# Attention and MLP on one core: the scores of the 64 left-over keys of two pairs in quarters of the TensorE array in full float32, with one sigmoid; copies of x by two engines, stores one step later

## The chip, the cores and the metric

The kernel runs on 1 core of one Trainium2 chip. The metric is the device time of one execution, in microseconds (us). TensorE (PE) does matmuls, with its weight loads shown apart as PEld; VectorE is DVE, ScalarE is ACT, GpSimd is POOL, and SyncE (SP) issues every DMA of this kernel, in one queue.

## The reference, cut to what matters

```python
def _attn_ref(q, k, v):                     # q, k, v: (8, 12, 448, 64) float32
    S = q.shape[2]
    scale = 1.0 / np.sqrt(q.shape[-1])
    scores = scale * np.matmul(q, k.transpose(0, 1, 3, 2)) - np.log(S)
    attn = 1.0 / (1.0 + np.exp(-scores))    # sigmoid, no row sum
    return np.matmul(attn, v).astype(np.float32)

def _moe_ref(x, w_in, w_out):               # x: (3584, 768), from the heads side by side
    h = x @ w_in                            # (768, 2048)
    r = np.maximum(h, 0.0)
    g = r * r
    return (g @ w_out).astype(np.float32)   # (2048, 768)
```

## The kernel before

The work has two stages. The first is the attention of 8 x 12 heads, taken two heads at a time: 48 pairs (b, p), numbered n = 0 to 47. The second is the two matrix products of the MLP, in four groups of two batches (`gemm1`, `gemm2`, lines 398 and on); each group splits its operands into blocks and multiplies seven combinations of them in place of eight. The order of all instructions is the order of the code: nothing is rescheduled, and every engine takes its instructions in that order.

**One pair.** `load_pair` brings q and k of both heads, transposed, into one tile x of 128 partitions: 64 rows of head 0 and 64 rows of head 1, then a half with the 448 queries and a half with the 448 keys. `split_pair` (lines 200 and 201) makes from it on DVE a rounded copy qh and the remainder ql. `scores` takes the 448 keys in blocks of 128, so three blocks (t = 0 to 2) and one of 64 left-over keys (t = 3; KR = 64). For each block line 215 issues three products (qh with qh, ql with qh, qh with ql) for each of the two heads. Head j uses the array's rows j x 64 to j x 64 + 63, so that the products of the two heads can run beside each other. Then one ACT instruction (line 223) turns the block of both heads into sigmoids. For t = 3 only 64 partitions are used, and the sigmoids go into one half of a tile `rest` that two neighbouring pairs share. The score tiles rotate through three PSUM buffers (`bufs=3`), so the fourth block of a pair needs the buffer of its first.

`attn_v` (line 231) multiplies the sigmoids of the three full blocks with v in full float32, head j into the output columns j x 64 and on. `attn_v_rest` (line 240) adds the left-over keys of two pairs at once: four products of 64 rows by 64 columns, one in each quarter of the array, again in full float32. Its result stands in a PSUM tile `pav`, of which there are two, one for the even and one for the odd pair. `put_x` copies pav to SBUF (line 249 on DVE, line 247 on ACT, which before the change only the very last pair uses) and returns the store to DRAM (line 253). For the first two batches (KEPT = 2) there is no store, the copy is kept.

**One step n.** `step(ps, n)` issues, in this order: the load of pair n + 4 (and of v for two pairs when n is even); when n is even, the copies of pairs n - 2 and n - 1 and their stores; the split of pair n + 2; the scores of pair n + 1; attn_v of pair n; when n is odd, attn_v_rest of pairs n - 1 and n; then a piece of the weights' work. So each even step on PE begins with the scores of an odd pair, straight after an attn_v_rest, and each odd step with the scores of an even pair.

**The weights' work** runs beside the attention. `weights(k)` is called for k = 0 to 48, spread over steps 0 to 44, twice in steps 0, 11, 22 and 33. A third of the calls hold `sums` (lines 155 to 158 on DVE, then two stores, lines 160 and 161), two thirds `convert_join` (lines 139, 140 and 143 on DVE, line 146 on POOL) and two thirds `convert_words` (lines 134 and 135 on ACT). From step 28 on, `PIECES` adds operands of the first MLP group (lines 259, 260 and 285).

Of the kernel before, what the change touches and what calls it, by code (L numbers as in the profile page):

```python
# [8 lines left out]
F32 = mybir.dt.float32  # L9
# [4 lines left out]
AF = mybir.ActivationFunctionType  # L14
# [3 lines left out]
B, H, S, D = 8, 12, 448, 64  # L18
DM, DFF = H * D, 2048
P = 128  # L20
NP = H // 2

NT, KR = S // P, S % P
# [5 lines left out]
SCALE = 1.0 / math.sqrt(D)  # L29
NEG_LOG_S = -math.log(S)  # L30
# [28 lines left out]
def sigmoid_attention_relu2_mlp(  # L59
# [42 lines left out]

    nc = tc.nc

    sb = ctx.enter_context(tc.tile_pool(name="sb", bufs=2))

    def op2(name, dtype=F32):
        return sb.tile([P, 2, S], dtype, tag="op2", bufs=N2, name=name)  # L110

    def op1(name, dtype=F32):
        return sb.tile([P, S], dtype, tag="op1", bufs=N1, name=name)

    def wide(name, dtype=F32):
        return sb.tile([P, PH, HALF], dtype, tag="w", bufs=NW, name=name)
# [20 lines left out]
    def convert_join(t, w):  # L137
        wb = w.bitcast(I32)
        nc.vector.tensor_scalar(out=w, in0=w, scalar1=WORD_MIN, scalar2=WORD_MAX, op0=ALU.max, op1=ALU.min)
        nc.vector.tensor_scalar(  # L140
            out=wb, in0=wb, scalar1=3, scalar2=0x3FFFFFFF, op0=ALU.logical_shift_left, op1=ALU.bitwise_and
        )
        nc.vector.scalar_tensor_tensor(  # L143
            out=wb, in0=t.bitcast(I32)[:, :, 1], scalar=-(1 << 30), in1=wb, op0=ALU.bitwise_and, op1=ALU.bitwise_or
        )
        nc.gpsimd.tensor_tensor(out=wb, in0=wb, in1=t.bitcast(I32)[:, :, 0], op=ALU.add)  # L146

    def sums(m, i, a, s):

        if m == 0:  # L150
            a21, a22, a11, a12 = (a[:, n] for n in range(4))
        else:
            a22, a12, a11, a21 = (a[:, n] for n in range(4))
        s2, s3, s4, s1 = (s[:, n] for n in range(4))
        nc.vector.tensor_add(out=s1, in0=a21, in1=a22)
        nc.vector.tensor_sub(out=s2, in0=s1, in1=a11)
        nc.vector.tensor_sub(out=s3, in0=a11, in1=a21)
        nc.vector.tensor_sub(out=s4, in0=a12, in1=s2)
        to = (w1, w2)[m][i]
        nc.sync.dma_start(out=to[:, 0:3], in_=a[:, 1:4] if m == 0 else a[:, 0:3])  # L160
        nc.sync.dma_start(out=to[:, 3:7], in_=s)

    def load_weights(sources, name):

# [28 lines left out]
    def load_v(b, d):  # L193
        vt = op2(f"v_{b}_{d}").rearrange("p a s -> p (a s)").rearrange("p (t d) -> p t d", d=P)
        nc.sync.dma_start(out=vt, in_=v[b, d])
        return vt
# [4 lines left out]
        nc.vector.tensor_sub(out=lo, in0=x, in1=hi.bitcast(F32))  # L201
        return hi, lo

    def scores(ps, b, p, x, rest):


        out = []
        for t in range(NT + 1):
            sc = ps.tile([P, 2, 512], F32, tag="sc", bufs=3, name=f"sc_{b}_{p}_{t}")[:, :, :S]
            keys = P if t < NT else KR  # L210
            ks = slice(t * P, t * P + keys)
            for n, (kp, qp) in enumerate(((0, 0), (1, 0), (0, 1))):
                for j in range(2):
                    rows = slice(j * D, (j + 1) * D)
                    nc.tensor.matmul(  # L215
                        sc[:keys, j], x[kp][rows, 1, ks], x[qp][rows, 0], start=(n == 0), stop=(n == 2)
                    )
            if t < NT:
                at = op2(f"at_{b}_{p}_{t}")
                out.append(at)  # L220
            else:
                at = rest[p % 2 * KR : (p % 2 + 1) * KR]
            nc.scalar.activation(at, sc[:keys], AF.Sigmoid, bias=NEG_LOG_S, scale=SCALE)  # L223
        return out

    def attn_v(ps, b, p, at, vt):
        pav = ps.tile([P, 512], F32, tag="pav", bufs=2, name=f"pav_{b}_{p}")[:, :S]
        for t in range(NT):
            for j in range(2):
                columns = slice(j * D, (j + 1) * D)  # L230
                nc.tensor.matmul(  # L231
                    pav[columns], vt[:, p % 2 * NT + t, columns], at[t][:, j], start=(t == 0), stop=False
                )
        return pav
# [9 lines left out]
    def put_x(b, p, pav, scalar=False):  # L244
        x = op1(f"xo_{b}_{p}")
        if scalar:
            nc.scalar.copy(out=x, in_=pav)
        else:
            nc.vector.tensor_copy(out=x, in_=pav)  # L249
        if b < KEPT:  # L250
            kept[b, p] = x
            return lambda: None
        return lambda: nc.sync.dma_start(out=xd[b, p], in_=x)
# [69 lines left out]
    pairs = [(b, p) for b in range(B) for p in range(NP)]  # L323
    last = len(pairs) - 1
    todo = [(m, i) for m in range(2) for i in range(NI)]
    x, vt, xs, at, pav, f64, w, rest = {}, {}, {}, {}, {}, {}, {}, {}
    stores = []
    pieces = {}
    ops = {}

    def weights(k):

        j, h = divmod(k, 3)
        if h == 0 and j > 0:
            sums(*todo[j - 1], *w[j - 1])
        if j == len(todo):
            return
        if h == 0:  # L340
            w[j] = wide(f"a_{j}"), wide(f"s_{j}")
        halves = w[j][0].rearrange("p a n -> p (a n)")
        halves = halves[:, DM:], halves[:, :DM]
        if h > 0:
            convert_join(f64[j, h - 1], halves[h - 1])
            if j + 1 < len(todo):
                f64[j + 1, h - 1] = load_chunk(*todo[j + 1], h - 1)
        if h < 2:
            convert_words(f64[j, h], halves[h])
# [3 lines left out]
    def step(ps, n):  # L353

        if n + XA <= last:
            x[n + XA] = load_pair(*pairs[n + XA])
            if n % 2 == 0:
                b, p = pairs[n + XA]
                vt[n // 2 + XA // 2] = load_v(b, p // 2)
        if n % 2 == 0 and n > 0:  # L360
            for m in (n - 2, n - 1):
                store = put_x(*pairs[m], pav.pop(m))
                if n <= last - 3:
                    store()
                else:
                    stores.append(store)
        if n + SA <= last:
            xs[n + SA] = split_pair(*pairs[n + SA], x[n + SA])
        if n < last:
            next_scores(ps, n + 1)  # L370
        pav[n] = attn_v(ps, *pairs[n], at[n], vt[n // 2])
        if n % 2:
            attn_v_rest((pav[n - 1], pav[n]), rest[n // 2], vt[n // 2])
        for k in range(NK):
            if k * NWP // NK == n:
                weights(k)
        pieces_of(*PIECES.get(n, ()))

    def next_scores(ps, n):
        if n % 2 == 0:  # L380
            rest[n // 2] = op2(f"rest_{n // 2}")
        at[n] = scores(ps, *pairs[n], xs[n], rest[n // 2])

    def pieces_of(*names):
        for name in names:
            pieces[name]()
# [261 lines left out]
```

## Time and profile before

| | |
|---|---|
| runs of the kernel before, median | 1108.82 us (1104.78, 1108.82, 1116.4) |
| the profiled execution, own time | 1108.67 us |
| its span, first to last instruction | 1106.9 us |
| attention, first score product to first MLP product | 5.99 to 280.84 us |
| granted TensorE clock | 1.00 throughout |

The span leaves 1.8 us of the execution's own time outside. "Busy" of PE is modelled from the starts of the matmuls, so a busy PE is not one at its peak. In a timeline row the first number is the start in us from the beginning of the span, the second how long the row took, x the number of instructions merged, and brackets tell of idle time before it and what ended it. A matmul in full float32 shows as two records, so the four products of line 240 are x8.

### The profile page before, as it was taken

Reading aid. Unit: us, or ns where it says so; the run is one execution under the profiler, and the core shown is the slowest. Engines: PE = TensorE matmul, PEld = TensorE weight load, DVE = VectorE, ACT = ScalarE, POOL = GpSimd, SP = SyncE. Lnnn points to the kernel's source line nnn. Section 1 sums busy time; section 2 is a strip of 40 time slices with the busy share of each in tenths; the row PEclk is TensorE's granted clock in tenths of the full one; section 3 lists DMA queues with packets and bytes.
Section 4 is the critical chain, followed back from the end, with each engine's and each line's share of the span. In section 5 each row is a group of like instructions: output and inputs, shape, how many; then the busy total and the mean of one; then the engine's idle time right before and its main releaser. Section 6 shows DMA issues by size and latency. Waiting matters only on the chain.

```text
span 1106.9 us, 15055 instructions
## 1 busy us (share of the span) xinstructions
PE 1094.7 (99%) x5965; PEld 893.6 (81%) x5965; DVE 798.2 (72%) x879; ACT 617.0 (56%) x745; POOL 63.4 (6%) x36
## 2 busy tenths in 40 slices
PE   9999999999999999999999999999999999999998
PEld 4455544445799999999999999999999999999997
DVE  6888898999655699744558977355798945459951
ACT  6788788887534546533435655333556633346630
POOL 1222222221000000000000000000000000000000
PEclk9999999999999999999999999999999999999999
DMA  8879998897232433653233355423443642233441
GB/s 318 331 283 361 355 360 322 315 367 286 67 122 101 122 107 108 235 175 104 100 100 121 123 173 198 136 100 100 136 124 125 215 150 100 100 115 128 139 136 53
DMA packets 80134, 196.81 MB, mean 178 GB/s; under 512 B 6336, under 2 KB 54464, under 8 KB 80064
## 3 DMA queue, kind: packets, MB, share of 16 engines
q1 hardware_dynamic: 80064, 195.85, 50.5%
q8 instruction: 47, 0.77, 0.3%
q14 instruction: 23, 0.19, 0.1%
HBM read 154.53 MB, written 41.29 MB: 177 GB/s over the span
## 4 chain that ended last, share of the span: by engine, by line
PE 91%; ACT 4%; DVE 3%; issue 1%; DMA 0%; ACTq 0%; DVEq 0%
PE oa L395 21%; PE ha L395 21%; PE ob L395 11%; PE hb L395 10%; PE sc L215 8%; PE pav L231 8%; PE hc L395 5%; PE oc L395 5%; PE pav L240 2%; ACT at L223 1%; DVE ql L201 1%; ACT rest L223 1%; ACT f L135 1%; DVE qh L200 0%; PE warm_ps L562 0%
## 5 line engine op out<-in xcount | busy, mean ns | idle before, releaser
L181 DVE TENSOR_TENSOR w_1l<-w_1l,w_1h 128x1536 fp32r<-128x1536 f32 x58 | 101.8, 1755 | 87.5 <-ACT w_1h L180 85.3
L223 ACT ACTIVATE at<-sc 128x896 f32<-128x896 f32 x144 | 121.6, 921 | 51.6 <-PE sc L215 51.4
L422 ACT COPY s<-ha 128x448 f32<-128x448 f32 x96 | 50.9, 532 | 163.7 <-PE ha L395 155.2
L231 PE MATMUL pav<-at,v 128*64 128x448 f32 x576 | 118.6, 547 | 1.1 <-DVE xo L249 1.1
L180 ACT CAST w_1h<-w_1l 128x1536 fp32r<-128x1536 f32 x58 | 85.9, 1480 | 23.8 <-DMA w_1l<-w 23.7
L231 PEld LDWEIGHTS pav<-at,v 128*64 128x64 f32 x576 | 37.2, 136 | 63.2 <-issue 58.7
L215 PE MATMUL sc<-qh 64*128 64x448 f32 (+1 forms) x384 | 77.2, 399 | 4.7 <-ACT at L223 4.7
L146 POOL TENSOR_TENSOR a<-a,f 128x768 int32<-128x768 int32 x32 | 63.2, 1976 | 198.6 <-DVE a L143 135.8
L215 PEld LDWEIGHTS sc<-qh 64*128 64x128 f32 (+1 forms) x384 | 33.3, 170 | 50.9 <-ACT at L223 16.3
L180 ACT CAST w_0h<-w_0l 128x1536 fp32r<-128x1536 f32 x28 | 41.5, 1481 | 55.3 <-DMA w_0l<-w 55.3
L201 DVE TENSOR_TENSOR ql<-x,qh 128x896 fp32r<-128x896 f32 x48 | 71.1, 1480 | 1.6
L455 DVE TENSOR_TENSOR g<-hb,s 128x448 f32<-128x448 f32 x32 | 19.9, 623 | 71.1 <-PE hb L395 71.1
L215 PE MATMUL sc<-qh,ql 64*128 64x448 f32 (+1 forms) x384 | 70.2, 362 | 0.3 <-DVE ql L201 0.3
L215 PE MATMUL sc<-ql,qh 64*128 64x448 f32 (+1 forms) x384 | 70.3, 362 | 0.0
L181 DVE TENSOR_TENSOR w_0l<-w_0l,w_0h 128x1536 fp32r<-128x1536 f32 x28 | 49.2, 1757 | 24.4 <-ACT w_0h L180 24.1
L180 ACT CAST w_5h<-w_5l 128x1152 fp32r<-128x1152 f32 x31 | 35.9, 1160 | 47.3 <-DMA w_5l<-w 47.2
L181 DVE TENSOR_TENSOR w_5l<-w_5l,w_5h 128x1152 fp32r<-128x1152 f32 x31 | 42.0, 1353 | 21.9 <-ACT w_5h L180 21.9
L418 DVE SCALAR_TENSOR_TENSOR g<-g 128x896 f32<-128x896 f32 x48 | 52.2, 1088 | 1.0
L223 ACT ACTIVATE rest<-sc 64x896 f32<-64x896 f32 x48 | 43.7, 909 | 0.6
L249 DVE COPY xo<-pav 128x448 f32<-128x448 f32 x47 | 27.1, 618 | 19.5 <-PE pav L240 19.5
L200 DVE CAST qh<-x 128x896 fp32r<-128x896 f32 x48 | 36.4, 759 | 5.6 <-DMA x<-qk 5.6
L511 DVE TENSOR_TENSOR o<-ob,t 128x448 f32<-128x448 f32 x24 | 14.9, 619 | 35.2 <-PE ob L395 29.0
(628 smaller groups left out, 3025.7 us busy)
## 6 DMA issues: line engine op xcount, KB each, us to landing
w_1l<-w SPq DMA_DIRECT2D x58, 768.0 KB, 4.3
x<-qk SPq DMA_DIRECT2D x48, 448.0 KB, 7.1
w_0l<-w SPq DMA_DIRECT2D x28, 768.0 KB, 4.7
f<-w_in SPq DMA_DIRECT2D x16, 768.0 KB, 7.5
w<-s SPq DMA_DIRECT2D x16, 768.0 KB, 4.2
f<-w_out SPq DMA_DIRECT2D x16, 768.0 KB, 6.9
w_5l<-w SPq DMA_DIRECT2D x31, 384.0 KB, 3.9
v<-v SPq DMA_DIRECT2D x24, 448.0 KB, 7.2
```

The source lines that it names most:

```text
L146: nc.gpsimd.tensor_tensor(out=wb, in0=wb, in1=t.bitcast(I32)[:, :, 0], op=ALU.add)
L180: nc.scalar.copy(out=hi, in_=raw)
L181: nc.vector.tensor_sub(out=lo, in0=raw, in1=hi.bitcast(F32))
L200: nc.vector.tensor_copy(out=hi, in_=x)
L201: nc.vector.tensor_sub(out=lo, in0=x, in1=hi.bitcast(F32))
L215: nc.tensor.matmul(sc[:keys, j], x[kp][rows, 1, ks], x[qp][rows, 0], start=(n == 0), stop=(n == 2))
L223: nc.scalar.activation(at, sc[:keys], AF.Sigmoid, bias=NEG_LOG_S, scale=SCALE)
L231: nc.tensor.matmul(pav[columns], vt[:, p % 2 * NT + t, columns], at[t][:, j], start=(t == 0), stop=False)
L249: nc.vector.tensor_copy(out=x, in_=pav)
L395: nc.tensor.matmul(out, a[:, c], b, start=first and n == 0, stop=last and n == 2, skip_group_check=True)
L418: nc.vector.scalar_tensor_tensor(out=t, in0=t, scalar=0.0, in1=t, op0=ALU.max, op1=ALU.mult)
L422: nc.scalar.copy(out=s, in_=banks["a", i])
```

## The change

The scores of the 64 left-over keys leave `scores`. They are computed once for two pairs, behind the scores of the odd pair, by `scores_rest`: four products, pair r into output partitions r x 64 and on, head j from rows j x 64 and on, from the unsplit x in full float32, one product each in place of three. One sigmoid over 128 partitions takes the place of two over 64. In `step` the copy of pair n - 2 goes to ACT and stays at the front, the copy of pair n - 1 stays on DVE and moves behind the weights' work. The weights' stores are issued in the step after their sums; the stores of x are issued in the odd step after their copies, and those of pairs 42 to 47 wait for a place in the first MLP group.

```diff
-        to = (w1, w2)[m][i]
-        nc.sync.dma_start(out=to[:, 0:3], in_=a[:, 1:4] if m == 0 else a[:, 0:3])
-        nc.sync.dma_start(out=to[:, 3:7], in_=s)
+
+        def store():
+            to = (w1, w2)[m][i]
+            nc.sync.dma_start(out=to[:, 0:3], in_=a[:, 1:4] if m == 0 else a[:, 0:3])
+            nc.sync.dma_start(out=to[:, 3:7], in_=s)
+
+        return store
...
-    def scores(ps, b, p, x, rest):
-
+    def sigmoid(name, sc):
+        at = op2(name)
+        nc.scalar.activation(at, sc, AF.Sigmoid, bias=NEG_LOG_S, scale=SCALE)
+        return at
+
+    def scores(ps, b, p, x):
 
         out = []
-        for t in range(NT + 1):
+        for t in range(NT):
...
+    def scores_rest(ps, d, xs):
+
+        sc = ps.tile([P, 2, 512], F32, tag="sc", bufs=3, name=f"sr_{d}")[:, :, :S]
+        for r, x in enumerate(xs):
+            for j in range(2):
+                rows = slice(j * D, (j + 1) * D)
+                nc.tensor.matmul(
+                    sc[r * KR : (r + 1) * KR, j], x[rows, 1, NT * P :], x[rows, 0], start=True, stop=True
+                )
+        return sigmoid(f"rest_{d}", sc)
...
-            sums(*todo[j - 1], *w[j - 1])
+            ready.append(sums(*todo[j - 1], *w[j - 1]))
...
+        for waiting in (ready, stores) if n % 2 and n < last - 2 else (ready,):
+            for store in waiting:
+                store()
+            waiting.clear()
         if n % 2 == 0 and n > 0:
-            for m in (n - 2, n - 1):
-                store = put_x(*pairs[m], pav.pop(m))
-                if n <= last - 3:
-                    store()
-                else:
-                    stores.append(store)
+            stores.append(put_x(*pairs[n - 2], pav.pop(n - 2), True))
...
+        if n % 2 == 0 and n > 0:
+            stores.append(put_x(*pairs[n - 1], pav.pop(n - 1)))
         pieces_of(*PIECES.get(n, ()))
 
     def next_scores(ps, n):
-        if n % 2 == 0:
-            rest[n // 2] = op2(f"rest_{n // 2}")
-        at[n] = scores(ps, *pairs[n], xs[n], rest[n // 2])
+        at[n] = scores(ps, *pairs[n], xs[n])
+        if n % 2:
+            rest[n // 2] = scores_rest(ps, n // 2, (x[n - 1], x[n]))
```

On PE, at step 18: the scores of the odd pair (b 3, p 1), the name's first numbers being b, p and the block of keys, and what follows. Before:

```order
L215 MATMUL sc_3_1_2_1290<-qh_3_1_1199 128x448 x2
L215 MATMUL sc_3_1_2_1290<-qh_3_1_1199,ql_3_1_1200 128x448 x2
L215 MATMUL sc_3_1_2_1290<-ql_3_1_1200,qh_3_1_1199 128x448 x2
L215 MATMUL sc_3_1_3_1299<-qh_3_1_1199 64x448 x2
L215 MATMUL sc_3_1_3_1299<-qh_3_1_1199,ql_3_1_1200 64x448 x2
L215 MATMUL sc_3_1_3_1299<-ql_3_1_1200,qh_3_1_1199 64x448 x2
L231 MATMUL pav_3_0_1307<-at_3_0_0_1211,v_3_0_1010 64x448 x2
```

And now, where sr_9 is the score tile of the left-over keys of pairs 18 and 19:

```order
L223 MATMUL sc_3_1_2_1187<-qh_3_1_1109 128x448 x2
L223 MATMUL sc_3_1_2_1187<-qh_3_1_1109,ql_3_1_1110 128x448 x2
L223 MATMUL sc_3_1_2_1187<-ql_3_1_1110,qh_3_1_1109 128x448 x2
L235 MATMUL sr_9_1196<-x_3_0_927 64x448 x2
L235 MATMUL sr_9_1196<-x_3_1_990 64x448 x2
L245 MATMUL pav_3_0_1203<-at_3_0_0_1120,v_3_0_929 64x448 x2
```

The six products of 64 keys behind the third block have become four, which read x itself; behind the scores of an even pair, where six stood too, nothing stands now.

On DVE, at step 20: xo are the copies of pairs 18 and 19, qh and ql the split of the pair two ahead, a_7 the weights' join. Before:

```order
L249 COPY xo_3_0_1387<-pav_3_0_1307 128x448
L249 COPY xo_3_1_1390<-pav_3_1_1362 128x448
L200 CAST qh_3_4_1393<-x_3_4_1258 128x896
L201 TENSOR_TENSOR ql_3_4_1394<-x_3_4_1258,qh_3_4_1393 128x896
L139 TENSOR_SCALAR a_7_1379<-a_7_1379 128x768
L140 TENSOR_SCALAR a_7_1379<-a_7_1379 128x768
L143 SCALAR_TENSOR_TENSOR a_7_1379<-f64_0_7_0_1254,a_7_1379 128x768
```

And now:

```order
L205 CAST qh_3_4_1280<-x_3_4_1159 128x896
L206 TENSOR_TENSOR ql_3_4_1281<-x_3_4_1159,qh_3_4_1280 128x896
L140 TENSOR_SCALAR a_7_1268<-a_7_1268 128x768
L141 TENSOR_SCALAR a_7_1268<-a_7_1268 128x768
L144 SCALAR_TENSOR_TENSOR a_7_1268<-f64_0_7_0_1155,a_7_1268 128x768
L263 COPY xo_3_1_1333<-pav_3_1_1253 128x448
```

The copy of pair 18 has left DVE, and that of pair 19 stands behind the split and the join.

On SP, at the same steps, the queue of transfers. Before:

```order
L190 DMA x_3_5_1320<-qk 128x896
L160 DMA w1<-a_6_1193 128x1152
L161 DMA w1<-s_6_1194 128x1536
L190 DMA x_4_0_1383<-qk 128x896
L195 DMA v_4_0_1385<-v 128x896
L253 DMA xd<-xo_3_0_1387 128x448
L253 DMA xd<-xo_3_1_1390 128x448
L122 DMA f64_1_0_0_1443<-w_out 128x1536
L190 DMA x_4_1_1447<-qk 128x896
```

And now:

```order
L195 DMA x_4_0_1272<-qk 128x896
L200 DMA v_4_0_1274<-v 128x896
L163 DMA w1<-a_6_1097 128x1152
L164 DMA w1<-s_6_1098 128x1536
L123 DMA f64_1_0_0_1329<-w_out 128x1536
L195 DMA x_4_1_1335<-qk 128x896
L267 DMA xd<-xo_3_0_1278 128x448
L267 DMA xd<-xo_3_1_1333 128x448
```

Loads of x and v that stood behind a store now stand ahead of it.

## Rows read from the trace of the kernel before

**Rows 1.** The page's head: busy us, share of the span, instructions

```profile
PE 1094.7 (99%) x5965; PEld 893.6 (81%) x5965; DVE 798.2 (72%) x879; ACT 617.0 (56%) x745; POOL 63.4 (6%) x36
```

**Rows 2.** Stretches: their length, each engine's busy us, PEclk, DMA share, GB/s

```profile
80.00:240.00 160.00, 156.24 (x1122) 78.77 (x1120) 145.46 (x194) 129.75 (x159) 39.99 (x21) 1.00 0.92 347
240.00:281.00 41.00, 39.57 (x279) 18.95 (x276) 35.47 (x49) 30.76 (x40) 6.04 (x3) 1.00 0.74 273
281.00:1107.00 826.00, 821.80 (x4032) 756.53 (x4031) 553.87 (x553) 394.00 (x474) 0.00 (x0) 1.00 0.39 128
```

**Rows 3.** Timeline of PE: both ends of the attention

```profile
5.99 0.47 PE L215 MATMUL sc<-qh 64*128 64x448 f32 x2
...
274.39 4.73 PE L231 MATMUL pav<-at,v 128*64 128x448 f32 x24 [0.63 <-DVE xo L249]
279.05 0.98 PE L240 MATMUL pav<-rest,v 64*64 64x448 f32 x8
280.84 0.44 PE L395 MATMUL ha<-x_0h,w_firsth 128*128 128x448 f32 x1 [0.80 <-DVE xo L249]
```

**Rows 4.** Timeline of PE: the end of step 17, steps 18 and 19

```profile
110.01 0.98 PE L240 MATMUL pav<-rest,v 64*64 64x448 f32 x8
110.92 0.47 PE L215 MATMUL sc<-qh 64*128 64x448 f32 x2
...
112.64 0.37 PE L215 MATMUL sc<-ql,qh 64*128 64x448 f32 x2
112.85 0.37 PE L215 MATMUL sc<-qh 64*64 64x448 f32 x2
...
113.26 0.36 PE L215 MATMUL sc<-ql,qh 64*64 64x448 f32 x2
113.55 2.48 PE L231 MATMUL pav<-at,v 128*64 128x448 f32 x12
115.95 0.47 PE L215 MATMUL sc<-qh 64*128 64x448 f32 x2
...
121.07 0.98 PE L240 MATMUL pav<-rest,v 64*64 64x448 f32 x8
121.98 0.47 PE L215 MATMUL sc<-qh 64*128 64x448 f32 x2
```

**Rows 5.** Waits up to 470 us: who waited for whom, us in total, times, longest

```profile
PE sc L215 <- ACT at L223: 4.7, 5, 1.5
```

**Rows 6.** Timeline of PE, DVE and ACT at the start of step 23

```profile
138.10 0.47 PE L215 MATMUL sc<-qh 64*128 64x448 f32 x2
138.43 0.56 DVE L139 TENSOR_SCALAR a<-a 128x768 f32<-128x768 f32 x1 [0.45 <-ACT a L134]
139.62 0.96 DVE L143 SCALAR_TENSOR_TENSOR a<-f,a 128x768 int32<-128x768 int32 x1
140.70 2.52 ACT L223 ACTIVATE at<-sc 128x896 f32<-128x896 f32 x3
141.15 2.63 DVE L201 TENSOR_TENSOR ql<-x,qh 128x896 fp32r<-128x896 f32 x1
141.65 0.41 PE L215 MATMUL sc<-qh 64*64 64x448 f32 x2 [1.46 <-ACT at L223]
```

**Rows 7.** The page's groups of DVE: busy, mean ns of one, idle before

```profile
L201 DVE TENSOR_TENSOR ql<-x,qh 128x896 fp32r<-128x896 f32 x48 | 71.1, 1480 | 1.6
...
L249 DVE COPY xo<-pav 128x448 f32<-128x448 f32 x47 | 27.1, 618 | 19.5 <-PE pav L240 19.5
L200 DVE CAST qh<-x 128x896 fp32r<-128x896 f32 x48 | 36.4, 759 | 5.6 <-DMA x<-qk 5.6
```

**Rows 8.** Timeline of PE, DVE, ACT: step 34's late copies, the last copy

```profile
202.49 0.47 PE L215 MATMUL sc<-qh 64*128 64x448 f32 x2
...
205.44 1.15 DVE L249 COPY xo<-pav 128x448 f32<-128x448 f32 x2
...
280.13 0.53 ACT L247 COPY xo<-pav 128x448 f32<-128x448 f32 x1 [4.70 <-PE pav L240]
```

More of the change, by code (lines that the diff above doesn't have):

```diff
@@ L202, in split_pair @@
         return hi, lo
-    def scores(ps, b, p, x, rest):
+    def sigmoid(name, sc):
[3 more added lines that the diff above has]
+    def scores(ps, b, p, x):
         out = []
-        for t in range(NT + 1):
+        for t in range(NT):
             sc = ps.tile([P, 2, 512], F32, tag="sc", bufs=3, name=f"sc_{b}_{p}_{t}")[:, :, :S]
-            keys = P if t < NT else KR
-            ks = slice(t * P, t * P + keys)
+            ks = slice(t * P, (t + 1) * P)
             for n, (kp, qp) in enumerate(((0, 0), (1, 0), (0, 1))):
@@ L215, in scores @@
                     nc.tensor.matmul(
-                        sc[:keys, j], x[kp][rows, 1, ks], x[qp][rows, 0], start=(n == 0), stop=(n == 2)
+                        sc[:, j], x[kp][rows, 1, ks], x[qp][rows, 0], start=(n == 0), stop=(n == 2)
                     )
-            if t < NT:
-                at = op2(f"at_{b}_{p}_{t}")
-                out.append(at)
-            else:
-                at = rest[p % 2 * KR : (p % 2 + 1) * KR]
-            nc.scalar.activation(at, sc[:keys], AF.Sigmoid, bias=NEG_LOG_S, scale=SCALE)
-        return out
+            out.append(sigmoid(f"at_{b}_{p}_{t}", sc))
+        return out
+    def scores_rest(ps, d, xs):
[7 more added lines that the diff above has]
+        return sigmoid(f"rest_{d}", sc)
     def attn_v(ps, b, p, at, vt):
@@ L326, in sigmoid_attention_relu2_mlp @@
     x, vt, xs, at, pav, f64, w, rest = {}, {}, {}, {}, {}, {}, {}, {}
-    stores = []
+    ready, stores = [], []
     pieces = {}
@@ L359, in step @@
                 vt[n // 2 + XA // 2] = load_v(b, p // 2)
+        for waiting in (ready, stores) if n % 2 and n < last - 2 else (ready,):
+            for store in waiting:
+                store()
+            waiting.clear()
         if n % 2 == 0 and n > 0:
-            for m in (n - 2, n - 1):
-                store = put_x(*pairs[m], pav.pop(m))
-                if n <= last - 3:
-                    store()
-                else:
-                    stores.append(store)
+            stores.append(put_x(*pairs[n - 2], pav.pop(n - 2), True))
         if n + SA <= last:
```

## The prediction

> **What bounds the kernel now.** I read the page's head first: PE is busy 99% of the span [rows 1]. Busy ends of matmuls are modelled, so I read the distances between starts instead. The table by stretches comes next [rows 2]: the granted clock is 1.00, the 2.4 GHz level, in all of them; behind 281 us nothing that the change touches is left but six stores, and PE is busy 821.8 of 826 us. So the change is worth what it does to the attention, 5.99 to 280.84 us, 274.85 us long [rows 3].
>
> Inside it I read PE's timeline for two steps [rows 4]. Step 18 starts at 110.92, step 20 at 121.98: 11.06 us for two pairs. The reader is to see start after start with hardly a hole: nine pairs of products of full blocks in 1.93 us, then the left-over keys, where two slots take 113.26 - 112.85 = 0.41, so 0.205 each; then 0.09 more than a slot until attn_v starts at 113.55; 2.40 us of attn_v; at the end of two steps 0.91 us of attn_v_rest (110.01 to 110.92). PE's own instructions are the period, and the other engines matter where they make it wait.
>
> How much is that? The stage is 274.85. From it come 46 attn_v of 2.40 and the last two, 4.66 (274.39 to 279.05); 23 attn_v_rest of 0.91 and the last with its change to the MLP, 1.79 (279.05 to 280.84). That leaves 137.1 us for the scores of 48 pairs. At 2.63 each (110.92 to 113.55) they would take 126.2. So about 10.9 us are waits, spread unevenly. The table of waits gives their main kind: PE stood five times for a sigmoid, 4.7 us together [rows 5]. One such place shows how [rows 6]: step 22 has two calls of weights, so ACT comes to the sigmoids of the next pair only at 140.70 (2.52 for three, 0.84 each), and the fourth score block, which needs the buffer of the first, starts at 141.65 after 1.46 us of idling. The block began at 138.10; undisturbed it would have got there 1.93 later.
>
> **The change part by part.** *Products of the left-over keys.* Three slots go from every pair: 3 x 0.205 = 0.61 us. Behind an odd pair four full products come. The trace has their twin: line 240 also does four products of 64 by 64 with 448 columns in float32, one in each quarter, in 0.91 us with the change to the next form [rows 4]. Even pairs: 24 x -0.61 = -14.6. Odd pairs: 24 x (0.91 - 0.61) = +7.2. Sum -7.4. Bounds: the cheapest row is that of the rounded products, two slots for four products, 0.41, which would give 12 us more; the dearest is attn_v's, six products in 2.40, 0.40 each, four in 1.60, which costs 24 x 0.69 = 16.6 more. I take 0.91, same shape and same quarters.
>
> The changeover of the array has a rule against it. From 64 by 128 to 64 by 64 the start moves 0.21 (112.64 to 112.85), a slot like any other; into attn_v it costs 0.09 [rows 4]. The Trainium skill, TensorEngine Tiling (Array Packing), section Key Properties, says that a change of tiling mode drains the engine. There is one change less in two steps now. By the rule each would cost the 0.09 of attn_v's, and the sum would be 2.2 us lower; by the row nothing.
>
> *Sigmoids and copies.* ACT loses one sigmoid of about 0.84 per two steps and gains one copy of 0.53 [rows 8]: -0.31, while the period shrinks by 0.31 as well. ACT is busy 129.75 of 160 us [rows 2], so its load stays about 81%. What matters is which waits end. An even pair has three score blocks for three buffers now, so a late sigmoid no longer stops it in its own block. The wait of rows 6, and those like it after steps 0 and 28, go. An odd pair still needs a fourth buffer, 2.02 after its start (1.93 and 0.09), and has the 0.53 copy ahead of its first sigmoid. Where ACT is late there, after the double calls of steps 11 and 33, I leave 0.7 each.
>
> DVE loses 0.62 per two steps [rows 7]. More, it loses a wait: it stood 19.5 us for attn_v_rest before those copies. Its second copy is due later: attn_v of step n + 1 needs it, at 2.93 + 2.40 + 2.02 = 7.35 us after the start T of an even step (2.93 is 2.02 with 0.91). On DVE it stands behind a split (759 + 1480 ns [rows 7]), a join (138.43 to 140.58, 2.15 [rows 6]) and takes 0.62: 5.0 if DVE is on time. Queued behind the waiting copy are the next split and the scores that read it, so DVE's order keeps PE's two-step slack. In step 22 the join waits for words of its own step: it ended at 140.58, 7.5 after that step's start at 133.07 (138.10 less 2.63 and 2.40), then 0.62: 0.8 late, charged once.
>
> *Of the 10.9 us of waits I leave 4.3*: 1.4 after the double calls, 0.8 for step 22, 0.4 in the last odd pair (0.63 before for DVE [rows 3], now for ACT), 0.4 at the start, and about 1.3 in small ones. Gain 6.6. Bounds: none goes (0), or all (10.9).
>
> *Stores and queue.* SP issues the weights' stores one step later, those of x in odd steps, six of them in the MLP. Loads that stood behind a store go ahead. I cost this at nothing: after the start DVE waits for loads of x no more (5.6 us in all [rows 7]), so an earlier load hides behind the split's place in DVE's order. What it costs if the queue fills up is a rival below. The scores also read x itself, so its buffer comes free later; the loads are two steps ahead, which covers it.
>
> Sum: -7.4 - 6.6 = -14.0. Against the profiled execution's own time, 1108.67, it gives 1094.7. The span's 1.8 us outside stay. The median of the runs, 1108.82, is the same time, so I forecast 1094.7 for that too. About 1% is what a measurement of this kernel can tell from no change; 1% is 11 us, so the line is 1097.7.
>
> **The rivals.** *The waits move instead of going.* PE gets its -7.4, and ACT, as loaded as before, stops the odd block instead. For it: the odd block keeps four tiles on three buffers and gets a copy first. Against: the buffer comes free about when wanted even in the undisturbed steps of rows 4. Time 1108.67 - 7.4 = 1101.3.
>
> *Transfers bound the middle.* From 80 to 240 us the DMA share is 0.92 [rows 2], 147 us of transfers. That stretch would get 14.0 x 160 / 274.85 = 8.1 us of the gain, and the share would be 147 / 152 = 0.97. If it can't rise above 0.92, that gain is lost: 1102.8. Against: loads leave the queue earlier.
>
> *The quarters don't run beside each other.* Two at a time is attn_v's rate: 1094.7 + 16.6 = 1111.3, no change. One at a time takes twice 1.60, that is 2.29 more than 0.91 each time: 1149.7. The row against both is line 240 with its 0.91. The Trainium skill, FP8 and Floating Point Precision, section TensorE Precision Notes, says that true float32 takes four passes through the array. By it four products, one after the other, would be sixteen slots, 3.28 us, and the change a loss of about 43 us; the 0.91 for four disagrees unless all quarters work at once.
>
> *Slower: the second copy comes too late in every even step.* Place: attn_v of the odd pair, which needs its PSUM tile. In step 34 DVE stood 2.95 late (205.44 against 202.49 [rows 8]). If it stood so always, the copy would end at 2.95 + 5.0 = 7.95, 0.6 late; with a split slowed to 2.63 in place of 1.48 [rows 6] 1.75 late. Price: 23 x 1.75 = 40, so 1135. It decides from 0.6 us per two steps, 23 x 0.6 = 14. Against: the 19.5 us that DVE stood idle at just this place.
>
> **How the numbers follow.** The forecast's chance is 0.66, with 1090 to 1099 as its own range; 0.56 of it lies below 1097.7. Waits that move 0.12, transfers 0.10, quarters 0.06, late copy 0.06. Some 0.04 of the first two would still come out below 1097.7. Faster by over 1%: 0.60; within 1%: 0.34, with the two-at-a-time case in it; slower: 0.06. The range takes in the first two rivals and ends at 1105; below it reaches to 1090, where nearly all waits go or each change of tiling costs 0.09.
>
> **What would show it.** Right: PE's starts in two steps 10.7 apart; sr tiles written by eight records within 0.98; an even pair's scores 2.02 from start to attn_v; no idling before an even pair's last block; ACT's copy directly behind attn_v_rest. Wrong: sr records in pairs 0.4 apart; attn_v waiting for line 263; DVE waiting for x; a DMA share at 1.0 through the middle with PE idle. The forecast falls if the attention ends later than about 270 us.

## The result, and the profile after

The changed kernel takes 1092.25 us (median of 6 runs) against 1108.05 (6 runs of the kernel before): the ratio is 0.985, 95% interval [0.981, 0.989], so it is faster by about 1.5%. In a second comparison it was 1092.7 (4 runs) against 1105.45 (23 runs), 0.988 [0.985, 0.991], 12.75 us. The first profiled execution of the changed kernel was a slow one, 1108.05 us with an attention of 262.19, so the rows below are from the profile taken with the second comparison; its own time is 1095.86 us, its span 1094.1.

The page's head of the changed kernel, to be read beside [rows 1]:

```profile
PE 1084.1 (99%) x5869; PEld 882.8 (81%) x5869; DVE 800.0 (73%) x856; ACT 608.5 (56%) x744; POOL 63.6 (6%) x36
```

Its table of stretches, beside [rows 2]; the attention now ends at 268 us:

```profile
80.00:240.00 160.00, 157.17 (x1120) 75.89 (x1118) 152.94 (x189) 132.59 (x170) 40.70 (x21) 1.00 0.93 350
240.00:268.00 28.00, 27.27 (x188) 12.20 (x184) 23.63 (x31) 19.11 (x26) 3.98 (x2) 1.00 0.68 250
268.00:1094.00 826.00, 821.69 (x4032) 756.70 (x4032) 553.67 (x554) 395.20 (x474) 0.00 (x0) 1.00 0.39 128
```

The MLP is as long as before, 826 us. All that was gained lies ahead of it. DVE is busier in the middle than before (152.94 against 145.46 us), and the transfers, at 0.92 before, run at 0.93.

PE's timeline of the changed kernel: the start, two steps, the end of the attention, beside [rows 3, 4].

```profile
6.12 0.54 PE L223 MATMUL sc<-qh 64*128 64x448 f32 x2
...
94.92 0.47 PE L223 MATMUL sc<-qh 64*128 64x448 f32 x2
...
96.65 0.37 PE L223 MATMUL sc<-ql,qh 64*128 64x448 f32 x2
96.94 0.98 PE L235 MATMUL sr<-x 64*64 64x448 f32 x8
97.86 2.48 PE L245 MATMUL pav<-at,v 128*64 128x448 f32 x12
100.26 0.47 PE L223 MATMUL sc<-qh 64*128 64x448 f32 x2
...
101.99 0.37 PE L223 MATMUL sc<-ql,qh 64*128 64x448 f32 x2
102.28 2.48 PE L245 MATMUL pav<-at,v 128*64 128x448 f32 x12
104.69 0.98 PE L254 MATMUL pav<-rest,v 64*64 64x448 f32 x8
105.60 0.47 PE L223 MATMUL sc<-qh 64*128 64x448 f32 x2
...
261.71 4.73 PE L245 MATMUL pav<-at,v 128*64 128x448 f32 x24
266.37 0.98 PE L254 MATMUL pav<-rest,v 64*64 64x448 f32 x8
268.16 0.44 PE L410 MATMUL ha<-x_0h,w_firsth 128*128 128x448 f32 x1 [0.80 <-DVE xo L263]
```

Two steps take 105.60 - 94.92 = 10.68 us, 11.06 before. The four products of the left-over keys (L235) stand once in them, 96.94 to 97.86, 0.92 long; an even pair's scores take 102.28 - 100.26 = 2.02. The attention lasts 268.16 - 6.12 = 262.04 us in place of 274.85: 12.81 less, and the two profiled executions differ by just that, 1108.67 - 1095.86.

I took this apart by the starts of all 48 blocks of scores, each counted up to the start of the attn_v behind it, so that a wait of that attn_v is in it too. Nothing else changed: attn_v is 110.67 us for 46 pairs in both traces. Before, the score blocks took 136.75: 48 undisturbed ones at 2.63 make 126.24, and 10.51 are waits. After, they take 123.94: 48 at 2.021 and 24 times 0.912 make 118.90, and 5.04 are waits. So the products gave 7.3 and the waits 5.5.

| waits, us | before | after |
|---|---|---|
| first two pairs | 0.58 | 0.35 |
| step 1 / 3 | 1.70 / - | - / 0.37 |
| step 12 | 0.54 | 0.63 |
| steps 23 / 25 | 1.67 / - | 0.47 / 0.25 |
| step 29 | 1.46 | - |
| steps 34 / 35 | 0.99 / 0.60 | 0.63 / 1.63 |
| step 39 | 0.44 | 0.50 |
| step 46 | 0.78 | 0.16 |
| all others, 0.13 and less each | 1.75 | 0.05 |

What DVE and PE wait for now, from the table of waits up to 470 us, beside [rows 5] (us in total, times, longest):

```profile
DVE xo L263 <- PE pav L254: 4.0, 1, 4.0
...
PE pav L245 <- DVE xo L263: 2.0, 5, 0.7
...
PE sr L235 <- ACT at L211: 1.1, 2, 0.6
```

An even pair's block stops for no sigmoid any more. In its place attn_v waits five times for the second copy. Two such places, steps 23 and 35, in the timeline of DVE, POOL and PE, the first beside [rows 6]:

```profile
132.05 0.56 DVE L140 TENSOR_SCALAR a<-a 128x768 f32<-128x768 f32 x1 [2.69 <-ACT a L135]
...
134.12 0.62 DVE L263 COPY xo<-pav 128x448 f32<-128x448 f32 x1
...
134.79 1.72 PE L245 MATMUL pav<-at,v 128*64 128x448 f32 x8 [0.40 <-DVE xo L263]
...
195.76 2.02 POOL L147 TENSOR_TENSOR a<-a,f 128x768 int32<-128x768 int32 x1 [7.50 <-DVE a L144]
196.11 2.62 DVE L206 TENSOR_TENSOR ql<-x,qh 128x896 fp32r<-128x896 f32 x1
...
198.78 0.47 PE L223 MATMUL sc<-qh,ql 64*128 64x448 f32 x2 [0.58 <-DVE ql L206]
...
200.70 0.62 DVE L263 COPY xo<-pav 128x448 f32<-128x448 f32 x1
...
201.38 2.10 PE L245 MATMUL pav<-at,v 128*64 128x448 f32 x10 [0.68 <-DVE xo L263]
```

In step 23 the copy stands behind a join that waited 2.69 us for ACT's words. In step 35 DVE is late altogether: the split's subtraction, 2.62 us long beside POOL's part of a join, stops the scores, and then the copy behind the next join stops attn_v.

The groups of DVE and ACT up to 269 us, beside [rows 7, 8]:

```profile
L206 DVE TENSOR_TENSOR ql<-x,qh 128x896 fp32r<-128x896 f32 x48 | 78.5, 1636 | 1.8
L205 DVE CAST qh<-x 128x896 fp32r<-128x896 f32 x48 | 45.7, 952 | 6.6 <-DMA x<-qk 6.6
L263 DVE COPY xo<-pav 128x448 f32<-128x448 f32 x24 | 14.8, 618 | 4.0 <-PE pav L254 4.0
L261 ACT COPY xo<-pav 128x448 f32<-128x448 f32 x24 | 12.9, 537 | 23.4 <-PE pav L254 23.4
```

The wait for attn_v_rest has moved from DVE (19.5 us) to ACT (23.4), which has the time. The split takes 1636 + 952 ns on average, 0.35 us more than before; the last section shows from what.

### The profile page after: what moved, and what is told of

It is laid out like the page before. It is cut to its first block, busy times and chain, and to the rows that moved or that the text cites. A ratio compares the mean times of both kernels' runs of the same rounds, so it can differ in the third digit from the quotient of the medians.

```text
span 1106.3 us, 14825 instructions
## 1 busy us (share of the span) xinstructions
PE 1096.6 (99%) x5869; PEld 882.7 (80%) x5869; DVE 800.9 (72%) x856; ACT 608.6 (55%) x744; POOL 63.5 (6%) x36
## 4 chain that ended last, share of the span: by engine, by line
PE 90%; DVE 5%; ACT 3%; DMA 1%; issue 0%; SPq 0%; ACTq 0%
PE oa L410 22%; PE ha L410 21%; PE ob L410 11%; PE hb L410 11%; PE pav L245 7%; PE oc L410 5%; PE hc L410 5%; PE sc L223 5%; DVE ql L206 2%; PE pav L254 1%; PE sr L235 1%; ACT at L211 1%; DMA x<-qk 1%; DVE a L144 1%; DVE qh L205 1%; DMA f<-w_out 1%
## 5 line engine op out<-in xcount | busy, mean ns | idle before, releaser
L185 ACT CAST w_1h<-w_1l 128x1536 fp32r<-128x1536 f32 x58 | 85.9, 1480 | 22.3 <-DMA w_1l<-w 22.0
L206 DVE TENSOR_TENSOR ql<-x,qh 128x896 fp32r<-128x896 f32 x48 | 78.5, 1635 | 1.8
L223 PE MATMUL sc<-qh 64*128 64x448 f32 x288 | 58.2, 401 | 0.0
L223 PEld LDWEIGHTS sc<-qh 64*128 64x128 f32 x288 | 27.0, 184 | 35.3 <-issue 12.0
L223 PE MATMUL sc<-qh,ql 64*128 64x448 f32 x288 | 52.6, 362 | 0.6 <-DVE ql L206 0.6
L433 DVE SCALAR_TENSOR_TENSOR g<-g 128x896 f32<-128x896 f32 x48 | 52.3, 1090 | 1.0
L223 PE MATMUL sc<-ql,qh 64*128 64x448 f32 x288 | 52.6, 362 | 0.0
L205 DVE CAST qh<-x 128x896 fp32r<-128x896 f32 x48 | 45.7, 952 | 5.4 <-DMA x<-qk 5.4
L464 ACT ACTIVATE g<-ha 128x448 f32<-128x448 f32 x32 | 17.4, 545 | 37.9 <-PE ha L410 37.9
L410 PE MATMUL oa<-o_0h,w_0l 128*128 128x448 f32 x96 | 35.3, 368 | 0.0
```

The source lines that it names most:

```text
L185: nc.scalar.copy(out=hi, in_=raw)
L205: nc.vector.tensor_copy(out=hi, in_=x)
L223: nc.tensor.matmul(sc[:, j], x[kp][rows, 1, ks], x[qp][rows, 0], start=(n == 0), stop=(n == 2))
L410: nc.tensor.matmul(out, a[:, c], b, start=first and n == 0, stop=last and n == 2, skip_group_check=True)
L433: nc.vector.scalar_tensor_tensor(out=t, in0=t, scalar=0.0, in1=t, op0=ALU.max, op1=ALU.mult)
```

## The experiments

The first question was which part of the change does it. Theory: the left-over scores alone. The rivals: the copies, or the stores with the order of the queue.

**e1_after**: the changed kernel as it is.

> The changed kernel as it is, for a second profile. Theory A (products of the left-over keys give 7.4 us, the ended waits for sigmoids another 6 to 9): 1092 us; attention ends near 265 to 268 us, two steps are 10.7 us apart, an even pair's scores take 2.02 us to attn_v, the four full products 0.91. Theory B (the MLP stage behind the attention became shorter too): attention ends near 268 us and the rest of the span is 2 us or more under the 826 us of before.

Measured: 1092.7, ratio 0.988 [0.985, 0.991], as theory A had it; its profile is the one shown above. Theory B falls, the MLP is no shorter.

**e2_rest**: the kernel before with the left-over scores changed, and nothing else.

```diff
...
-        at[n] = scores(ps, *pairs[n], xs[n], rest[n // 2])
+        at[n] = scores(ps, *pairs[n], xs[n])
+        if n % 2:
+            rest[n // 2] = scores_rest(ps, n // 2, (x[n - 1], x[n]))
```

> Only the scores of the left-over keys are changed (quarters, full float32, one sigmoid); copies and stores stay as before. Theory A (products and fewer score tiles do it, copies and stores are worth about nothing): 1092 to 1096 us. Theory C (the freed DVE queue, by the copies, ends the waits): only the products' 7.4 us, so about 1101 us.

Measured: 1093.76, ratio 0.989 [0.987, 0.991], as theory A had it. Its attention is 263.59 us long, 1.55 more than with all three parts. The copies, both on DVE here, stop attn_v, by 1.79 us in step 34 and at the end by 0.56:

```profile
262.36 4.73 PE L240 MATMUL pav<-at,v 128*64 128x448 f32 x24 [0.56 <-DVE xo L258]
```

**e3_copies**: the kernel before, with only the copies moved.

```diff
...
-            for m in (n - 2, n - 1):
-                store = put_x(*pairs[m], pav.pop(m))
...
+            store = put_x(*pairs[n - 2], pav.pop(n - 2), True)
...
+        if n % 2 == 0 and n > 0:
+            store = put_x(*pairs[n - 1], pav.pop(n - 1))
...
         pieces_of(*PIECES.get(n, ()))
```

> Only the copies of x are moved (even pair on ACT at the front, odd pair on DVE behind the weights' work, each store right behind its copy); scores as before. Theory A: within 2 us of before, rather slower, since ACT gets 0.53 us per two steps and the fourth score tile still waits for ACT: 1107 to 1112 us. Theory C: 5 us or more faster than before, 1103 us or less.

Measured: 1105.86 beside 1105.45, ratio 0.999 [0.998, 1.001]; attention 274.14 us, 0.7 less than before. That is within theory A's 2 us, though not slower as it leaned to, and far from theory C.

**e4_stores**: the kernel before, with only the stores issued later.

```diff
...
+        for waiting in (ready, stores) if n % 2 and n < last - 2 else (ready,):
+            for store in waiting:
+                store()
+            waiting.clear()
...
```

> Only the stores are issued later (weights one step, x in odd steps); copies and scores as before. Theory A: no change, within 2 us of before. Theory D (loads held up behind stores cost PE time in a way that the waits do not name): 3 us or more faster than before.

Measured: 1105.95, ratio 1.000 [0.998, 1.001]; attention 274.96 us, as before. So the left-over scores carry the gain. The stores do nothing, and the copies are worth 0.7 us alone and, with the stores, 1.5 beside the new scores, below what these times can tell apart.

The next question: why do the new scores gain, by the work on PE, by the buffers, or by ACT's lighter load?

**e5_two_sigmoids**: the changed kernel with ACT's saving taken back.

```diff
-        return sigmoid(f"rest_{d}", sc)
+        at = op2(f"rest_{d}")
+        for r in range(2):
+            part = slice(r * KR, (r + 1) * KR)
+            nc.scalar.activation(at[part], sc[part], AF.Sigmoid, bias=NEG_LOG_S, scale=SCALE)
+        return at
```

> The changed kernel with the one sigmoid of the left-over keys split into two of 64 partitions each, so ACT has about 0.84 us more to do in two steps (24 x 0.84 = 20 us over the attention); PE's products and the number of score tiles stay. Theory A (PE's own instructions are the period; what ended the waits is that an even pair no longer needs a fourth score buffer): 1093 to 1096, at most 3 us above the changed kernel's 1092.7. Rival B (the waits went because ACT has less to do): the 5.5 us of waits that went come back, 1098 or more.

Measured: 1100.43, 7.7 more than the changed kernel (on another chip, where the kernel before took 1105.89); ratio to the kernel before 0.994 [0.992, 0.996]. By the time theory A fell. Where the 7.7 lie is another matter. The first MLP product stands at 271.14 and the attention is 265.03 us long, only 3.0 more. The rest is in the MLP, whose code is the same. PE's and ACT's rows at the one large hole there:

```profile
271.14 0.44 PE L414 MATMUL ha<-x_0h,w_firsth 128*128 128x448 f32 x1 [0.80 <-DVE xo L267]
...
480.78 1.15 ACT L185 CAST w_5h<-w_5l 128x1152 fp32r<-128x1152 f32 x1 [8.29 <-DMA w_5l<-w]
...
482.42 0.47 PE L414 MATMUL ha<-xt_1h,w_1h 128*128 128x448 f32 x1 [2.23 <-ACT s L441]
```

ACT stood for a load of weights, the snapshot that PE needed stood behind it, and PE idled for 2.23 us. Between the starts of the two products around that hole stand 2.59 us, and some of the products behind it are slow (the last section has them): together this costs 4.0 us by this one profile. All six runs of this kernel are as long (1099.28 to 1101.42); whether the others have that hole too, and why the load came late, is not shown.

In the attention, the table of waits has the second copy above the rest:

```profile
PE pav L249 <- DVE xo L267: 3.8, 6, 1.4
```

In the changed kernel this row has 2.0 us. No even pair's block stops for a sigmoid here either, although ACT is busy 143.29 of 160 us in the middle (132.59 in the changed kernel, 129.75 before). So what ended those stops is the missing fourth buffer, and theory A is right for the attention, to the edge of its bound. ACT's saving is worth 3.0 us, but for the most part in another place: the joins on DVE wait longer for ACT's words (6.9 us in place of 4.2 up to the end of the attention), and the copies behind them come later.

**e7_four_tiles**: the kernel before, its fourth tile made by one full float32 product per head.

```diff
-            for n, (kp, qp) in enumerate(((0, 0), (1, 0), (0, 1))):
+            for n, (kp, qp) in enumerate(((0, 0), (1, 0), (0, 1)) if t < NT else ((2, 2),)):
...
```

> The kernel before (1105.45) with one change: the fourth score tile of every pair is made by one full float32 product per head from the unsplit x, two quarters of the array in use, in place of three rounded products per head; tiles, sigmoids, copies and stores as before. Theory A (a float32 product of 448 columns lasts about 0.82 us whatever else runs, and only products in different quarters run side by side): two products take what four do, 0.91 with the change of form, against 0.70 before (2.63 less 1.93), so 48 x 0.21 = 10 us more, 1113 to 1116. Rival B (products in quarters go by number, four records in half the time of eight): 0.41 + 0.09 = 0.50, so 48 x 0.20 = 10 us less, 1095 to 1097, and the pairing of two pairs would not have been needed for the products' part of the gain.

Measured: 1115.53, ratio 1.009 [1.006, 1.012], as theory A had it. PE's timeline of one pair:

```profile
110.08 0.37 PE L215 MATMUL sc<-ql,qh 64*128 64x448 f32 x2
110.38 0.97 PE L215 MATMUL sc<-x 64*64 64x448 f32 x4
111.28 2.48 PE L231 MATMUL pav<-at,v 128*64 128x448 f32 x12
```

Two products take 111.28 - 110.38 = 0.90, what four take in the changed kernel. A full float32 product is four slots of 0.205 long, 0.82, with 0.09 to the next form, whether two quarters run or four. The Trainium skill, FP8 and Floating Point Precision, section TensorE Precision Notes, says that true float32 takes four passes through the array. This trace agrees, with its 0.90 for two products and 0.91 for four. Half full, the array loses: the exchange of three rounded products for a full one pays only because two pairs fill all four quarters.

**e8_two_wide**: the changed kernel with its left-over products 128 columns wide; it leaves out the separate left-over scores of the two pairs and adds up 128 keys of both in their place.

```diff
-                rows = slice(j * D, (j + 1) * D)
-                nc.tensor.matmul(
-                    sc[r * KR : (r + 1) * KR, j], x[rows, 1, NT * P :], x[rows, 0], start=True, stop=True
-                )
+                rows = slice(j * D, (j + 1) * D)
+                nc.tensor.matmul(sc[:, j], x[rows, 1, S - P :], x[rows, 0], start=(r == 0), stop=(r == 1))
```

> The changed kernel with the four products of the left-over keys made over 128 columns of the array instead of 64 (keys 320 to 447, both pairs added up in one tile), so that only two can run beside each other, and the array changes its form one time less in two steps. Its scores of the left-over keys are not those of the reference. Theory A (quarters are worth their number): attn_v's rate, 0.40 for each of four products, 1.60 in place of 0.91, 24 x 0.69 = 16.6 more, less up to 3 us of waits that the longer block covers: 1106 to 1110, the time of the kernel before. Rival B (0.91 is set by something else, such as the loads of x or the waits): within 2 us of 1092.7.

Measured: 1107.42, ratio 1.001 [0.999, 1.004]: the gain is gone, as theory A said.

```profile
101.77 0.37 PE L223 MATMUL sc<-ql,qh 64*128 64x448 f32 x2
101.97 1.74 PE L235 MATMUL sr<-x 64*128 64x448 f32 x8
103.64 0.60 PE L243 MATMUL pav<-at,v 128*64 128x448 f32 x2
```

Two at a time, the four products take 1.67. And the first of them starts 0.20 after the last rounded one, where in the changed kernel it is 96.94 - 96.65 = 0.29: going over from rounded products to full float32 costs nothing in the same form of the array, and 0.09 into another form.

The last question was whether the 5.0 us of waits that are left can be had, in a version faster than the changed kernel.

**e9_copy_ahead**: the changed kernel with the second copy ahead of the weights' work.

```diff
+        if n % 2 == 0 and n > 0:
+            stores.append(put_x(*pairs[n - 1], pav.pop(n - 1)))
         for k in range(NK):
             if k * NWP // NK == n:
                 weights(k)
-        if n % 2 == 0 and n > 0:
-            stores.append(put_x(*pairs[n - 1], pav.pop(n - 1)))
```

> The changed kernel with the second copy of x on DVE issued ahead of the weights' work of its step instead of behind it. In the profile of the changed kernel attn_v stood five times for that copy, 2.0 us in all, behind a join that itself waited for ACT's words. Theory A: these waits go, 1 to 2 us less, 1090.7 to 1091.7. Rival B (the copy now stands ahead of work that DVE needs in time, and waits for attn_v_rest there as both copies did before the change): the next split comes late instead, 0 to 2 us more, 1092.7 to 1094.7.

Measured: 1093.25, ratio 0.988 [0.986, 0.991], no gain, as rival B had it. attn_v's waits for the copy went, but PE's waits for the split rose from 0.6 to 2.8 us, and the attention is 262.72 us long. Of the 48 subtractions of the split 28 are slow ones of about 2.6 us here, 17 in the changed kernel (the last section says what makes them slow).

**e10_after_shift** and **e11_before_shift**: the doubled calls of weights moved, in the changed kernel and in the kernel before.

```diff
-            if k * NWP // NK == n:
+            if (k * NWP + 8) // NK == n:
```

> The changed kernel with the doubled calls of weights moved by two or more steps: calls 2 and 3, 14 and 15, 26 and 27, 38 and 39 share a step (steps 2, 13, 24, 35) in place of 0 and 1, 12 and 13, 24 and 25, 36 and 37 (steps 0, 11, 22, 33). A doubled step then holds one set of words on ACT in place of two, and a join beside the sums on DVE. Theory A (the waits left behind doubled steps come from ACT's two sets of words): the 0.63 in step 12, the 0.63 in step 34 and the 0.47 in step 23 go, 1.7 us less, 1090.5 to 1092. Rival B (DVE, loaded as before or more in a doubled step, makes the second copy late there): 1093 to 1096.

> The same move of the doubled calls in the kernel before. In its profile the waits next to doubled calls are 1.70 us in step 1, 0.54 in step 12, 1.67 in step 23 and 1.59 in steps 34 and 35, 5.5 of 10.5 us in all. Theory A (ACT's two sets of words in one step are their cause, and the fourth score buffer is where they are paid): 3 to 5.5 us less than the kernel before, 1100.5 to 1103 against 1105.5 to 1106; then a good part of what the change gained in waits could have been had by this move alone. Rival B (the waits move to the new doubled steps): within 1 us of the kernel before.

Measured: 1093.17, ratio 0.988 [0.985, 0.990], and 1105.87, ratio 0.999 [0.997, 1.001]. In the changed kernel the waits of steps 12, 23 and 34 are gone, but 3.0 us stand in steps 37 to 39 behind the new doubled step 35; the attention is 261.06 us, 1.0 less. So the three waits went as theory A had it, and DVE's lateness came as rival B had it, in whose range the time lies. In the kernel before the waits moved entirely (274.66 us), as rival B had it. Its rows at step 36 show how:

```profile
213.36 0.56 DVE L155 TENSOR_TENSOR s<-a 128x384 f32<-128x384 f32 x1 [2.07 <-POOL a L146]
...
216.03 2.48 PE L231 MATMUL pav<-at,v 128*64 128x448 f32 x12 [1.31 <-DVE xo L249]
```

A doubled step with a join and sums makes DVE wait for POOL, which ends the join, and the copies behind come late.

**e12_shift_ahead**: the edits of e9 and e10 together.

> The changed kernel with both: doubled calls moved as in the run before, and the second copy on DVE ahead of the weights' work. Theory A (copy ahead takes away attn_v's waits for the copy, 2.0 us; it brought waits for the split behind doubled steps, which the move thins out): 1089 to 1091.5, below the changed kernel. Rival B (the split stays late): 1092 to 1094.

Measured: 1094.48, ratio 0.989 [0.986, 0.991]; attention 262.83. This is above the range of either theory; the two edits do not add up to a gain. The second copy stops nothing any more, but the split stays late, as rival B had it: in steps 37 and 38, behind the doubled step 35, PE waits for both halves of it. The worse of the two, step 38:

```profile
214.40 0.47 PE L223 MATMUL sc<-qh 64*128 64x448 f32 x2 [1.26 <-DVE qh L205]
215.43 0.74 PE L223 MATMUL sc<-qh,ql 64*128 64x448 f32 x2 [0.56 <-DVE ql L206]
```

**e13_early_doubles**: the changed kernel with all doubled calls ahead of step 28.

```diff
-            if k * NWP // NK == n:
+            if k - sum(k > m for m in (2, 8, 14, 20)) == n:
```

> The changed kernel with all four doubled calls ahead of step 28, where DVE's work on the first MLP group begins: calls 2 and 3, 8 and 9, 14 and 15, 20 and 21 share steps 2, 7, 12 and 17, and every step from 18 to 44 has one call. The profile of the run with doubled steps 2, 13, 24 and 35 shows 3.0 us of waits for DVE in steps 37 to 39, behind the last of them, and none behind the other three. Theory A (doubled steps with one set of words cost PE nothing where DVE has no pieces of the MLP to make): the attention ends its waits but for about 1 us at both ends, 262.1 becomes 258 to 259.5 us, and the time is 1089 to 1091. Rival B (the steps 36 to 40 are late through the pieces themselves, or the weights' loads, now earlier, fill the queue): attention 260.5 or more, the time 1092 to 1094, as the changed kernel's.

Measured: 1094.94, on a chip where the kernel before took 1108.38, ratio 0.990 [0.987, 0.993]; attention 262.81. The time is above both ranges, the attention in rival B's. The waits of steps 36 to 40 went, as theory A had it (0.16 are left in step 39), and one place ate it all, step 13. DVE's and PE's rows there:

```profile
80.06 0.56 DVE L156 TENSOR_TENSOR s<-a 128x384 f32<-128x384 f32 x1 [2.04 <-POOL a L147]
...
82.07 0.61 DVE L263 COPY xo<-pav 128x448 f32<-128x448 f32 x1
...
82.74 4.17 PE L245 MATMUL pav<-at,v 128*64 128x448 f32 x12 [2.90 <-DVE xo L263]
```

Step 12 is doubled and even, so its second copy stands behind DVE's wait for POOL. PE stood for 2.90 us, and the attn_v behind it took 86.84 - 82.74 = 4.10 in place of 2.41. But a doubled even step does not do this by itself: step 2 of this run and step 24 of e10 are such steps too, with the same wait for POOL of 2.0 us, and attn_v was on time. There DVE came to its split over 3 us ahead of PE's start of the step; in step 12 it came 0.3 behind it. Without the 2.98 + 1.69 of this place the attention would be 258.1 us; whether other early steps would bring that was not tried. None of these versions was measured faster than the changed kernel; e10's attention, 1.0 us shorter, does not show in its time.

## Why the prediction was right

The forecast was 1094.7 us, with 1090 to 1099 as its own range; 1092.25 was measured, faster by over 1% as the likeliest case said.

- **The products, -7.4.** Measured -7.3. The twin in line 240 was the right row: 0.912 for the four products, 2.021 for an even pair's scores. e7 and e8 show why: a product is four slots long whether one or three others run beside it, and four quarters run at once. The period was forecast as 10.7 and is 10.68.
- **The changeover of the array.** The Trainium skill, TensorEngine Tiling (Array Packing), section Key Properties, says that a change of tiling mode drains the engine. At the 0.09 of attn_v's change for each, an estimate, that would have made the sum 2.2 lower. That saving did not come, the even pair's scores took the 2.02 forecast; but e8 shows that the rule isn't idle here: from rounded products into full ones of another form the change costs 0.09, which the forecast had in its 2.93 for an odd pair's scores.
- **The waits, -6.6.** Measured -5.5; this is the term that was mis-sized, by 1.1. Of its parts the 1.4 behind the double calls of steps 11 and 33 came as 1.26 (0.63 twice), the 0.8 for step 22 as 0.47, the start's 0.4 as 0.35, the last odd pair's as 0.16. The small ones, 1.3 left by forecast, became 0.05, but steps 3, 25, 35 and 39 have 2.75, above all the 1.63 of step 35. There the rival "the second copy comes too late" is at work, as it was priced: a split of 2.63, the join, then the copy. It happens five times for 2.0 us, not in every even step; its condition of 0.6 us per two steps was far from met. Of the 1.1, 0.4 lie in the trace before, which holds 10.5 us of waits and not 10.9 (attn_v takes 2.406, the sum had 2.40), and 0.7 in the 5.0 that are left in place of 4.3.
- **Which waits end.** The forecast put them on the even pair's fourth buffer, and those stops went (steps 1, 23 and 29), in e5 too, with ACT loaded more than before. But in e5 8.0 us are waits, only 2.5 less than before; the other 3.0 of the 5.5 need the lighter ACT, which the forecast had at nothing: it set ACT's saving of 0.31 against the shorter period and called its load unchanged. ACT's share of the middle was 0.81 and is 0.83 (132.59 of 160 us), and at that load 0.84 us per two steps more or less still count, through the joins and the copy behind them.
- **DVE's split.** The forecast took it as 759 + 1480 ns, the means of rows 7. The 1480 is no length that occurs: before, 36 subtractions take 1.09 us and 12 take 2.62 to 2.66. The changed kernel has 17 of the long ones, so its mean is 1636. Step 35's wait is such a long one.
- **Copies, stores and queue, 0.** By e3 and e4 right for each alone, within a quarter of a per cent. Beside the new scores they are worth 1.5 us of attention by the profiles, which the forecast did not see.
- **The rivals.** The waits did not just move, the transfers hold at 0.93 (in e2 0.96 with PE at its period), the quarters run side by side.
- **The base.** The sum stood against a profiled execution of 1108.67, and I took that for the median. 23 runs have 1105.45. The gain was forecast 1.2 too large and the base is 3.2 too high, so part of the good agreement is luck, two errors of opposite sign.

## What to carry to other kernels

In this kernel three rounded products of a half-used array are worth replacing by one full float32 product only where four such products fill the quarters of the array; half full, the same exchange loses. Read the price from an instruction of the same shape and form in the trace. A wait that is removed from one place of an engine's in-order list can be paid again by the next thing in that list, as in e9 to e13: count what stands behind it before moving work, and measure the stage, not the whole, when the gain is a tenth of a per cent. And look at the spread of an instruction's times before taking their mean as its price.

## What the runs showed that was not expected

The split's subtraction on DVE has two lengths, and which one it has goes with POOL's work. Its row in the kernel before and in the changed one, with the shortest, the median and the longest time in ns:

```profile
L201 DVE TENSOR_TENSOR ql<-x,qh x48: 1091/1093/2659, 4.6 to 268.1; 128x896 fp32r<-128x896 f32 x48
L206 DVE TENSOR_TENSOR ql<-x,qh x48: 1091/1093/2653, 4.7 to 256.9; 128x896 fp32r<-128x896 f32 x48
```

In these two traces, and in those of e2, e3, e4 and e9, every one that overlaps POOL's part of a join takes 2.56 to 2.67 us, POOL having begun first each time, and every other one takes 1.09. Before, 12 of 48 overlap, in the changed kernel and in e3 17, in e9 28. The cast ahead of it takes 0.61 to 0.63 us alone, and also where POOL begins after it. Where POOL began first, it takes up to 1.57 us before, and 2.01 to 2.13 us eleven times in the changed kernel. So moving the copies, which is all that e3 does, lets more splits fall beside POOL's work. That is where the split's longer mean comes from; how far it holds the changed kernel back was not tried.

The MLP, whose code is the same in all these kernels, takes between 822.0 and 826.1 us by the profiles used here, at a granted clock of 1.00, and 828.1 in e5 with its hole. Its 4032 matmuls start 0.2039 us apart on average in the profile of the kernel before and of the changed one, 0.2029 in that of e4: 4 us for nothing that the profile names. A gain of 12.8 us in the attention stands beside that.

A wait of PE can cost more than its length. Behind the 2.23 us of e5 nine matmuls in a row, 483.95 to 487.31, are 0.37 apart in place of 0.20, and the granted clock is 0.70 in that stretch; behind the 2.90 of e13 it is 0.77, and attn_v is 1.69 longer:

```profile
482.40:488.00 5.60, 5.58 (x20) 5.06 (x21) 2.54 (x3) 1.90 (x2) 0.00 (x0) 0.70 0.01 4
```

```profile
84.00:90.00 6.00, 6.00 (x38) 2.52 (x38) 5.90 (x7) 1.86 (x3) 2.02 (x1) 0.77 1.01 357
```

Of the two levels, 1.2 and 2.4 GHz, both stretches are at the lower one for a part. A hole of 1.46 us in the kernel before [rows 6] brought no such fall [rows 2], nor did one of 1.79 us in e2. But the length of one hole does not decide it: the 1.26 and 0.56 us of e12, close together, did.

```profile
212.00:218.00 6.00, 4.17 (x26) 2.72 (x26) 5.87 (x8) 1.74 (x3) 1.13 (x2) 0.78 1.02 382
```
